# Chunked attention into a GELU MLP: the first tile's V in runs of 512 bytes, with 32-key score and AV blocks

## The chip, the cores and the metric

The kernel runs on one core of one Trainium2 chip. Its time is the device time of one execution in microseconds (us). TensorE is called PE below, its weight loads PEld, VectorE DVE, ScalarE ACT, GpSimd POOL, and SyncE, which issues nearly all transfers, SP.

## The reference

Attention within chunks of 64 tokens, with no mask, and then an MLP with exact GELU over the 4608 tokens:

```python
batch, n_heads, seq, head_dim = (8, 8, 576, 64)
...
scores = scale * np.matmul(q_c, k_c.transpose(0, 1, 2, 4, 3))    # per chunk of 64 tokens
attn = np.exp(scores - max); attn = attn / sum(attn)
out = np.matmul(attn, v_c)
x = out.transpose(0, 2, 1, 3).reshape(B * S, H * D)              # 4608 x 512
h = x @ w_in                                                      # 4608 x 2048
g = 0.5 * h * (1.0 + erf(h * inv_sqrt2))
return g @ w_out                                                  # 4608 x 512
```

Inputs and output are f32 in HBM.

## The kernel before, in words

The 4608 tokens are cut into nine tiles of 512. Tiles 0 to 7 are the first 512 tokens of each batch entry (eight chunks), and the last tile holds the ninth chunk of all eight entries. In each tile attention gives x (four blocks `g` of 128 features, which are two heads each, by 512 tokens), then come the products with w_in (and GELU) and with w_out. Products are in bf16. From tile 1 on, the products use a scheme with seven block products for eight; tile 0 uses plain ones (`mm1_begin` L486, `mm1_slot` L471). Each engine runs its instructions in the order in which the program text issues them (the block under `manual_schedule`, L869). A buffer that is reused makes the writer wait for its last reader.

The change concerns tile 0, that is, L870 to L925. There are no earlier products to hide its attention behind. SP first issues four loads each of q and k (`load_qk`, L112, one pair of heads each), then four of V (`load_v_plain`, L142 to L145), then w_in in chunks (`load_w_in`, L836): the first two chunks in halves, each half in an instruction of its own. w_in's last chunk, w_out and the next tile's q, k and V follow (from L918).

A load puts f32 into a staging tile; POOL, DVE or ACT casts it to bf16 (`cast_qk` L158, `cast_v_plain` L147, `cast` L842). q and k arrive with four consecutive tokens per partition, V with one token per partition: its innermost run in HBM is one row of 64 f32, 256 bytes, and partition p of block n holds key 128 n + p for all heads.

The units of work for each pair of heads `g` are:

- `T[2g]`, `T[2g+1]` (`att_T`, L169): PE transposes q, then k; DVE copies qT and ACT copies kT out of PSUM.
- `att_S` (L371): 16 score matmuls with 64x64 tiles of the PE array (64 features by 64 keys, 64 queries moving). Its PSUM banks hold keys on partitions, one bank per head of the pair. ACT then takes the exponent (L381) into pT.
- The sums over keys are made in two ways. For g = 0 and 1 `att_sum` (L383) multiplies pT by a matrix of ones, so that each sum appears on 64 partitions; DVE transposes 32x32 blocks (L393), takes the reciprocal (L397) and transposes back while spreading it (L398). For g = 2 and 3 `att_sum_pe` (L410) makes one sum per query with queries on partitions (L416), DVE inverts (`inverse`), PE spreads by a product with the identity in f32 (`spread`, L428), and ACT copies to SBUF (L431).
- `att_av` (L434): V is the stationary operand, 64 keys by 64 features, and pT moves. The result for two pairs of heads lies in two PSUM banks, one for each parity `c` of the chunk.
- `att_x` (L445): DVE multiplies by the inverse sums into x (L450).

`keep_warm` (L859) adds matmuls on zeros between the steps. The order of it all is written out by hand (L876 to L917). After the two AV halves of the first four heads and the AV of the last four, `mm1_begin` computes three blocks of h: six matmuls on the first half of x, then six on the second (L491). Its weights are cast by POOL, ACT, POOL (L920 to L923), and DVE casts a fourth (L924). Then `mm1_slot` goes on alone (L481), one block of h after another.

Of the kernel before, what the change touches and what calls it, by code (L numbers as in the profile page):

```python
# [11 lines left out]
def kernel(  # L12
# [37 lines left out]
    ones_bd = consts.tile([P, P], bf16, name="ones_bd")  # L50
    nc.vector.memset(ones_bd[:], 0.0)
    nc.vector.memset(ones_bd[0:CH, 0:CH], 1.0)
    nc.vector.memset(ones_bd[CH:P, CH:P], 1.0)

    ones_r = consts.tile([P, 2], bf16, name="ones_r")
    nc.gpsimd.memset(ones_r[:], 0.0)
    nc.gpsimd.memset(ones_r[0:CH, 0:1], 1.0)
    nc.gpsimd.memset(ones_r[CH:P, 1:2], 1.0)
# [87 lines left out]

    def cast_v_plain(t, copy, ns=range(CT // 2)):  # L147
        st = tiles[t]
        if 0 in ns:
            st["v"] = ld.tile([P, H, CT // 2, D], bf16, tag="v", name="v_nat")  # L150
        for n in ns:
            copy(st["v"][:, :, n], st["vf"][:, :, n])
# [24 lines left out]
    def parity_blocks(ns=range(4)):  # L177

        for n in ns:
            for a in range(2):  # L180
                for r in range(2):
                    c = a ^ r
                    yield n, r, c, 2 * n + c, slice(CH * r, CH * (r + 1)), slice(CH * c, CH * (c + 1))
# [187 lines left out]
    def att_S(t, g):  # L371

        st = tiles[t]
        if g % 2 == 0:
            st["s_ps"] = [ps_at.tile([P, 2, CT // 2, CH], f32, tag="at", name="s_ps") for _ in range(2)]
        for n, r, c, i, rs, cs in parity_blocks():
            nc.tensor.matmul(st["s_ps"][r][cs, g % 2, n], st["kT", g][rs, i, :], st["qT", g][rs, i, :],
                             start=True, stop=True, tile_position=(CH * r, CH * c))
        st["pT", g] = work.tile([P, 2, CT // 2, CH], bf16, tag="pT", name="pT", bufs=4)
        for r in range(2):  # L380
            nc.scalar.activation(st["pT", g][:, r], st["s_ps"][r][:, g % 2], Act.Exp, scale=scale)  # L381

    def att_sum(t, g, later=False):  # L383
        pT = tiles[t]["pT", g]
        sum_ps = ps_at.tile([P, MT], f32, tag="at", name="sum_ps")
        for c in range(2):
            for r in range(2):
                nc.tensor.matmul(sum_ps[CH * r:CH * (r + 1)].rearrange("p (n c e) -> p n c e", c=2, e=CH)[:, :, c],
                                 ones_bd[:, CH * c:CH * (c + 1)], pT[:, r], start=True, stop=True,
                                 tile_position=(0, CH * r))  # L390
# [19 lines left out]
    def att_sum_pe(t, g):  # L410

        pT = tiles[t]["pT", g]
        sT = ps_at.tile([P, 2, MT // P // 2, 2], f32, tag="at", name="sT")
        for r in range(2):
            for m in range(2):
                nc.tensor.matmul(sT[:, r, m], pT[:, r, 2 * m:2 * m + 2].rearrange("p n e -> p (n e)"), ones_r[:],  # L416
                                 start=True, stop=True)
        rr = work.tile([P, 2, MT // P // 2, 2], f32, tag="rr", name="rr", bufs=2)
# [4 lines left out]
        def spread():  # L423
            rc_ps = ps_mm.tile([P, CT // 2, 2, CH], f32, tag="mm", name="rc_ps")
            for m in range(2):
                for c in range(2):
                    for r in range(2):
                        nc.tensor.matmul(rc_ps[CH * r:CH * (r + 1), 2 * m:2 * m + 2, c],  # L428
                                         rr[:, r, m, c:c + 1].to_broadcast([P, D]), ident_f[:],
                                         start=True, stop=True, tile_position=(0, CH * r))  # L430
# [3 lines left out]
    def att_av(t, g2, ns):  # L434

        st = tiles[t]
        pool, tag = ((ps_tp, "tp"), (ps_at, "at"))[g2]
        if 0 in ns:
            st["av", g2] = [pool.tile([P, 2, CT // 2, CH], f32, tag=tag, name="av_ps") for _ in range(2)]
        for g in (2 * g2, 2 * g2 + 1):  # L440
            for n, r, c, i, rs, cs in parity_blocks(ns):
                nc.tensor.matmul(st["av", g2][c][rs, g % 2, n], st["v"][cs, 2 * g + r, n, :], st["pT", g][cs, r, n],
                                 start=True, stop=True, tile_position=(CH * c, CH * r))

    def att_x(t, g2, c, ns):  # L445

        st = tiles[t]
        def part(p):
            return p.rearrange("p g (n c e) -> p g n c e", c=2, e=CH)[:, :, ns[0]:ns[-1] + 1, c]
        nc.vector.tensor_tensor(part(st["x"][:, 2 * g2:2 * g2 + 2]), st["av", g2][c][:, :, ns[0]:ns[-1] + 1],  # L450
                                part(st["rcs", g2][:]), op=mybir.AluOpType.mult)
# [417 lines left out]
    with tc.manual_schedule():  # L869
# [3 lines left out]
        load_v_plain(0)  # L873
# [6 lines left out]
        cast_v_plain(0, PO)  # L880
# [15 lines left out]
        keep_warm(1)  # L896
        att_S(0, 2)
        T[6]()
        r1 = att_sum(0, 1, True)
        T[7]()  # L900
        i2, p2 = att_sum_pe(0, 2)
        i2()
        att_S(0, 3)
# [4 lines left out]
        att_av(0, 0, (0, 1))  # L908
        for c in range(2):
            att_x(0, 0, c, (0, 1))  # L910
        p3()
        att_av(0, 0, (2, 3))
        for c in range(2):
            att_x(0, 0, c, (2, 3))
        att_av(0, 1, range(4))
        for c in range(2):
            att_x(0, 1, c, range(4))  # L917
# [168 lines left out]
```

## Time and profile before

| | |
|---|---|
| median of 3 runs | 274.69 us (274.37 to 274.96) |
| the profiled execution | 274.82 us |
| its span, from the first to the last instruction | 273.0 us |
| granted TensorE clock | 1.00 |
| busy in the span: PE, DVE, ACT, POOL | 260.3, 220.4, 181.8, 91.2 us |
| moved by DMA | 53.96 MB, mean 198 GB/s |

The profile is of one execution. Busy times overlap between engines, so they don't add up to the span. "Idle before" an instruction is the time in which its engine had nothing to do just ahead of it, and behind the arrow stands what ended the wait. In the chain of waits each piece is the work that released the next one; a transfer stands there from its issue to its landing. The ends of matmuls are modelled, and matmuls overlap. In a row of the timeline the first number is the start in us from the start of the span, the second the length of the group, and "x16" is how many instructions it holds.

### The profile page before, as it was taken

To read this page: it belongs to the slowest core of one execution; us is meant where nothing else is said; L and a number is where in the kernel's file an instruction comes from. 1 tells how busy PE (TensorE), PEld (TensorE's weight loads), DVE (VectorE), ACT (ScalarE), POOL (GpSimd) and SP (SyncE) were. 2 spreads that over 40 slices of the span, in tenths; PEclk is the share of its full clock that TensorE was granted. 3 is DMA by queue.
4 is the path that set the end of the run, shared out by engine and by line. 5 is a ranking of instruction groups with operands and counts; after the bars stand their busy time and mean duration, and the time that the engine had idled before them with its cause. 6 is when DMAs were issued, how large, how long until landed. Compare 5 with 4: busy or idle time off the path is not lost.

```text
span 273.0 us, 7454 instructions
## 1 busy us (share of the span) xinstructions
PE 260.3 (95%) x2984; PEld 187.3 (69%) x3009; DVE 220.4 (81%) x386; ACT 181.8 (67%) x353; POOL 91.2 (33%) x180
## 2 busy tenths in 40 slices
PE   8689999999999999999999999999999999999993
PEld 2454454486448644768887888788878887888782
DVE  2663586979796999999989998999899889945852
ACT  3557755788667966986679567946884787338700
POOL 2725667360460443370372355133510321000000
PEclk9999999999999999999999999999999999999999
DMA  6999999996999998999899796987983410130005
GB/s 202 258 359 405 396 394 246 242 268 151 347 222 241 279 176 181 273 231 188 231 265 248 219 249 93 237 192 155 251 121 86 143 41 2 38 111 7 4 0 154
DMA packets 118066, 53.96 MB, mean 198 GB/s; under 512 B 93456, under 2 KB 112912, under 8 KB 118032
## 3 DMA queue, kind: packets, MB, share of 16 engines
q1 hardware_dynamic: 117712, 52.97, 74.8%
q8 instruction: 23, 0.38, 0.6%
q10 hardware_dynamic: 320, 0.52, 0.5%
q14 instruction: 11, 0.09, 0.1%
HBM read 36.70 MB, written 9.44 MB: 169 GB/s over the span
## 4 chain that ended last, share of the span: by engine, by line
PE 80%; DVE 7%; SPq 4%; ACT 3%; DMA 3%; issue 1%; POOL 0%; ACTq 0%; DVEq 0%
PE y_ps L673 27%; PE h_Y L611 11%; PE h_ps L631 8%; PE h_Z L611 8%; PE h_X L611 8%; PE y_ps L771 6%; PE h_ps L481 5%; PE y_ps L795 4%; DMA arrival<-in_moe_w_in_dram 3%; SPq L145 2%; PE s_ps L230 1%; SPq L112 1%; DVE part L255 1%; DVE x L368 1%; ACT y_ps L701 1%
## 5 line engine op out<-in xcount | busy, mean ns | idle before, releaser
L611 PEld LDWEIGHTS <-w_in_s 128*128 128x128 bf16 x384 | 37.4, 98 | 6.8
L673 PEld LDWEIGHTS <-h_s 128*128 128x128 bf16 x384 | 37.0, 98 | 5.4 <-DVE h_s L513 0.8
L673 PE MATMUL y_ps<-w_t,h_s 128*128 128x256 bf16 x288 | 34.7, 273 | 0.3
L611 PEld LDWEIGHTS <-w_in_sb 128*128 128x128 bf16 x288 | 28.1, 98 | 8.3 <-issue 2.0
L208 POOL CAST v_nat<-arrival 128x1024 bf16<-128x1024 f32 x14 | 15.4, 1106 | 53.3 <-DMA arrival<-in_v_dram 46.7
L160 POOL CAST q_nat<-arrival 128x512 bf16<-128x512 f32 x33 | 22.2, 711 | 32.5 <-DMA arrival<-in_q_dram 24.2
L771 PE MATMUL y_ps<-w_out_sb,h 128*128 128x512 bf16 x137 | 31.5, 379 | 1.3 <-issue 1.0
L673 PEld LDWEIGHTS <-h 128*128 128x128 bf16 x288 | 28.2, 98 | 4.7
L631 PE MATMUL h_ps<-x,w_in_sb 128*128 128x512 bf16 x103 | 27.8, 379 | 0.7
L611 PE MATMUL h_Y<-x_t,w_in_s 128*128 128x256 bf16 x192 | 27.6, 272 | 0.0
L611 PE MATMUL h_X<-x,w_in_sb 128*128 128x256 bf16 x192 | 26.8, 273 | 0.0
L655 DVE TENSOR_TENSOR y<-h_Z,y 128x512 f32<-128x512 f32 x32 | 21.6, 680 | 5.8 <-PE h_Z L611 4.9
L160 POOL CAST k_nat<-arrival 128x512 bf16<-128x512 f32 x34 | 22.1, 684 | 11.6 <-DMA arrival<-in_k_dram 7.6
L771 PEld LDWEIGHTS <-h 128*128 128x128 bf16 x144 | 13.4, 98 | 15.6 <-issue 0.8
L673 PE MATMUL y_ps<-w_out_sb,h 128*128 128x256 bf16 x192 | 22.9, 273 | 0.0
L618 ACT ACTIVATE h<-y 128x512 bf16<-128x512 f32 x32 | 20.1, 628 | 1.7 <-DVE y L655 1.6
L867 ACT ACT_TABLE_LOAD x16 | 20.5, 1283 | 1.0 <-PEq L1070 0.7
L644 ACT COPY h_Y<-h_X 128x512 f32<-128x512 f32 x24 | 14.0, 584 | 10.5 <-PE h_X L611 10.4
L255 DVE TENSOR_REDUCE part<-pt 128x16 f32<-128x512 bf16 x28 | 19.2, 686 | 1.0
L633 ACT ACTIVATE h<-h_ps 128x512 bf16<-128x512 f32 x29 | 17.1, 595 | 2.6 <-PE h_ps L631 1.2
L307 DVE TENSOR_TENSOR x<-av_ps,rc 128x512 bf16<-128x512 f32 x28 | 18.0, 670 | 0.6
L631 PEld LDWEIGHTS <-w_in_sb 128*128 128x128 bf16 x116 | 11.4, 98 | 7.7
(129 smaller groups left out, 488.7 us busy)
## 6 DMA issues: line engine op xcount, KB each, us to landing
out_dram<-y_sb SPq DMA_DIRECT2D x32, 256.0 KB, 3.3
arrival<-in_q_dram SPq DMA_DIRECT2D x7, 1024.0 KB, 6.2
arrival<-in_k_dram SPq DMA_DIRECT2D x24, 256.0 KB, 6.2
arrival<-in_v_dram SPq DMA_DIRECT2D x42, 128.0 KB, 3.0
arrival<-in_moe_w_out_dram SPq DMA_DIRECT2D x4, 1024.0 KB, 12.4
arrival<-in_v_dram SPq DMA_DIRECT2D x8, 256.0 KB, 8.3
arrival<-in_moe_w_in_dram SPq DMA_DIRECT2D x4, 512.0 KB, 7.3
arrival<-in_moe_w_in_dram SPq DMA_DIRECT2D x2, 1024.0 KB, 10.4
```

The costliest lines, as they stand in the source:

```text
L160: copy(st[nm][:, g].rearrange("p j r d -> p r j d"), st[nm + "f"][:, 2 * g:2 * g + 2])
L208: copy(st["v"][:, r::2], st["vf"][:, r::2])
L255: nc.vector.tensor_reduce(st["part", g2][:, c, :, :, 0], pt[:].rearrange("p n e u -> p n u e"), axis=mybir.AxisListType.X, op=mybir.AluOpT ...
L307: nc.vector.tensor_tensor(x.rearrange("p n (e u) -> p n e u", u=2), st["av"][g2][c][:].rearrange("p n (e u) -> p n e u", u=2), st["rc", 2 ...
L611: nc.tensor.matmul(banks[g + name][:, i], lhs[:, kk, i], rhs[:, kk], start=fresh and i == kk == 0, stop=(kk == 1), skip_group_check=True)
L618: nc.scalar.activation(h[:, j:j + 2, m], src[:], Act.Gelu)
L631: nc.tensor.matmul(bank[:], w_in_sb[:, ks, f * P:(f + 1) * P], st["x"][:, ks, :], start=(ks == 0), stop=(ks == KS - 1))
L633: nc.scalar.activation(st["h"][:, f, :], bank[:], Act.Gelu)
L655: TT(sums[g, i][:], banks[g + "Z"][:], sums[g, i][:], op=add)
L673: nc.tensor.matmul(out[m], lhs[:, f, m * P:(m + 1) * P], rhs[:, f, :], start=fresh and f == 0 and (m == 0 or len(out) == 3), stop=(f == FH ...
L771: nc.tensor.matmul(y_ps[:], st["h"][:, f, ms * P:(ms + 1) * P], w_out_sb[:, f, :], start=(f == 0), stop=(f == FF - 1))
L867: nc.scalar.activation(act_scratch[:], rest[:, 0:1], func)
```

## The change

V of tile 0 is loaded with two consecutive tokens per partition (`load_v_pairs`), in four loads as before: two halves of the heads by two blocks of 256 tokens. A run in HBM is then 128 f32, 512 bytes. Partition p of block n holds keys 256 n + 2 p + j, for j = 0 and 1. A chunk of 64 keys therefore lies on 32 partitions, once for even and once for odd tokens, and the rest of the attention follows:

- `pair_blocks` takes the place of `parity_blocks`: 32 blocks instead of 16 for each pair of heads. The score matmuls take every other key of a chunk (32 of 64) as stationary operand, in 64x32 tiles of the array.
- `att_sum` has 16 matmuls of 128 columns in place of 4 of 256; even and odd keys are added up in PSUM. `att_sum_pe` keeps its four small matmuls and its eight of the spread; the inverse takes the same number of values.
- AV has 32x64 tiles and adds even and odd keys in PSUM: 128 matmuls for 64. Its result lies in four banks (one for each chunk position `c` of a block) that hold all four pairs of heads, where before each half of the pairs had two banks of its own.
- `att_x` is four multiplies of 256 elements for each two pairs, where before there were four of 256 and two of 512 in all.
- The constants of ones change (`ones_q`), and the cast V tile has rows of 65 elements, of which 64 are used.

In the order, the fourth pair's transposes (`T[6]`, `T[7]`) move ahead of the third pair's scores, and the fourth pair's scores ahead of the third pair's sums. The AV of the first four heads is no longer split around the last spread. Behind this point nothing changes.

```diff
...
     nc.vector.memset(rest[:], 0.0)
     ident = consts.tile([P, P], bf16, name="ident")
     make_identity(nc, ident)
-    ones_bd = consts.tile([P, P], bf16, name="ones_bd")
-    nc.vector.memset(ones_bd[:], 0.0)
-    nc.vector.memset(ones_bd[0:CH, 0:CH], 1.0)
-    nc.vector.memset(ones_bd[CH:P, CH:P], 1.0)
-
-    ones_r = consts.tile([P, 2], bf16, name="ones_r")
-    nc.gpsimd.memset(ones_r[:], 0.0)
-    nc.gpsimd.memset(ones_r[0:CH, 0:1], 1.0)
-    nc.gpsimd.memset(ones_r[CH:P, 1:2], 1.0)
+    Q4 = P // 4
+    ones_q = consts.tile([P, 4], bf16, name="ones_q")
+    nc.vector.memset(ones_q[:], 0.0)
+    for c in range(4):
+        nc.vector.memset(ones_q[Q4 * c:Q4 * (c + 1), c:c + 1], 1.0)
+
     ident_f = consts.tile([P, P], f32, name="ident_f")
     nc.gpsimd.tensor_copy(ident_f[:], ident[:])
     QD = P // G
...
         for n in range(CT // 2):
             nc.sync.dma_start(tiles[t]["vf"][:, :, n], v[t, :, P * n:P * (n + 1), :].rearrange("h key d -> key h d"))
 
+    def load_v_pairs(t):
+        tiles[t]["vf"] = stage_tile()[:].rearrange("p (h n e) -> p h n e", h=H, n=2)
+        for h0 in range(0, H, H // 2):
+            for n in range(2):
+                rows = v[t, h0:h0 + H // 2, 2 * P * n:2 * P * (n + 1), :]
+                nc.sync.dma_start(tiles[t]["vf"][:, h0:h0 + H // 2, n], rows.rearrange("h (p j) d -> p h (j d)", j=2))
+
+    def cast_v_pairs(t, copy):
+        st = tiles[t]
+        st["v"] = ld.tile([P, H, CT // 2, D + 1], bf16, tag="v", name="v_nat")
+        for h0 in range(0, H, H // 2):
+            for n in range(2):
+                copy(st["v"][:, h0:h0 + H // 2, 2 * n:2 * n + 2, :D],
+                     st["vf"][:, h0:h0 + H // 2, n].rearrange("p h (j d) -> p h j d", d=D))
+
     def cast_v_plain(t, copy, ns=range(CT // 2)):
         st = tiles[t]
         if 0 in ns:
...
         copy(xT.rearrange("p i (c j) -> p i c j", j=J), tp)
         tiles[t][nm + "T", g] = xT
 
-    def parity_blocks(ns=range(4)):
-
-        for n in ns:
-            for a in range(2):
-                for r in range(2):
-                    c = a ^ r
-                    yield n, r, c, 2 * n + c, slice(CH * r, CH * (r + 1)), slice(CH * c, CH * (c + 1))
+    def pair_blocks():
+
+        for n in range(2):
+            for j in range(2):
+                for c in range(4):
+                    for r in range(2):
+                        yield n, j, r, c, 4 * n + c, slice(CH * r, CH * (r + 1)), slice(Q4 * c, Q4 * (c + 1))
 
     ORDERED = (0, 1, 3)
 
...
         st = tiles[t]
         if g % 2 == 0:
             st["s_ps"] = [ps_at.tile([P, 2, CT // 2, CH], f32, tag="at", name="s_ps") for _ in range(2)]
-        for n, r, c, i, rs, cs in parity_blocks():
-            nc.tensor.matmul(st["s_ps"][r][cs, g % 2, n], st["kT", g][rs, i, :], st["qT", g][rs, i, :],
-                             start=True, stop=True, tile_position=(CH * r, CH * c))
+        for n, j, r, c, i, rs, cs in pair_blocks():
+            nc.tensor.matmul(st["s_ps"][r][cs, g % 2, 2 * j + n], st["kT", g][rs, i, j::2], st["qT", g][rs, i, :],
+                             start=True, stop=True, tile_position=(CH * r, Q4 * c))
         st["pT", g] = work.tile([P, 2, CT // 2, CH], bf16, tag="pT", name="pT", bufs=4)
         for r in range(2):
             nc.scalar.activation(st["pT", g][:, r], st["s_ps"][r][:, g % 2], Act.Exp, scale=scale)
...
     def att_sum(t, g, later=False):
         pT = tiles[t]["pT", g]
         sum_ps = ps_at.tile([P, MT], f32, tag="at", name="sum_ps")
-        for c in range(2):
-            for r in range(2):
-                nc.tensor.matmul(sum_ps[CH * r:CH * (r + 1)].rearrange("p (n c e) -> p n c e", c=2, e=CH)[:, :, c],
-                                 ones_bd[:, CH * c:CH * (c + 1)], pT[:, r], start=True, stop=True,
-                                 tile_position=(0, CH * r))
+        for c in range(4):
+            for j in range(2):
+                for r in range(2):
+                    nc.tensor.matmul(sum_ps[CH * r:CH * (r + 1)].rearrange("p (n c e) -> p n c e", c=4, e=CH)[:, :, c],
+                                     ones_q[:, c:c + 1].to_broadcast([P, CH]), pT[:, r, 2 * j:2 * j + 2], start=j == 0, stop=j == 1,
+                                     tile_position=(0, CH * r))
         t1 = work.tile([P, NB, 32], f32, tag=f"y_{1 + t}", name="t1", bufs=1)
         rc = rc_of(t, g).rearrange("p (n e) -> p n e", e=32)
         nc.vector.transpose(t1[:], sum_ps[:].rearrange("p (n e) -> p n e", e=32))
...
     def att_sum_pe(t, g):
 
         pT = tiles[t]["pT", g]
-        sT = ps_at.tile([P, 2, MT // P // 2, 2], f32, tag="at", name="sT")
+        sT = ps_at.tile([P, 2, 4], f32, tag="at", name="sT")
         for r in range(2):
-            for m in range(2):
-                nc.tensor.matmul(sT[:, r, m], pT[:, r, 2 * m:2 * m + 2].rearrange("p n e -> p (n e)"), ones_r[:],
-                                 start=True, stop=True)
-        rr = work.tile([P, 2, MT // P // 2, 2], f32, tag="rr", name="rr", bufs=2)
+            for j in range(2):
+                nc.tensor.matmul(sT[:, r], pT[:, r, 2 * j:2 * j + 2].rearrange("p n e -> p (n e)"), ones_q[:],
+                                 start=j == 0, stop=j == 1)
+        rr = work.tile([P, 2, 4], f32, tag="rr", name="rr", bufs=2)
 
         def inverse():
             nc.vector.reciprocal(rr[:], sT[:])
 
         def spread():
-            rc_ps = ps_mm.tile([P, CT // 2, 2, CH], f32, tag="mm", name="rc_ps")
-            for m in range(2):
-                for c in range(2):
-                    for r in range(2):
-                        nc.tensor.matmul(rc_ps[CH * r:CH * (r + 1), 2 * m:2 * m + 2, c],
-                                         rr[:, r, m, c:c + 1].to_broadcast([P, D]), ident_f[:],
-                                         start=True, stop=True, tile_position=(0, CH * r))
+            rc_ps = ps_mm.tile([P, 2, 4, CH], f32, tag="mm", name="rc_ps")
+            for c in range(4):
+                for r in range(2):
+                    nc.tensor.matmul(rc_ps[CH * r:CH * (r + 1), :, c], rr[:, r, c:c + 1].to_broadcast([P, D]), ident_f[:],
+                                     start=True, stop=True, tile_position=(0, CH * r))
             nc.scalar.copy(rc_of(t, g), rc_ps[:].rearrange("p n c e -> p (n c e)"))
         return inverse, spread
 
-    def att_av(t, g2, ns):
-
-        st = tiles[t]
-        pool, tag = ((ps_tp, "tp"), (ps_at, "at"))[g2]
-        if 0 in ns:
-            st["av", g2] = [pool.tile([P, 2, CT // 2, CH], f32, tag=tag, name="av_ps") for _ in range(2)]
+    def att_av(t, g2, n0=0, n1=2):
+
+        st = tiles[t]
+        if "av" not in st:
+            st["av"] = [pool.tile([P, G, 2, CH], f32, tag=tag, name="av_ps")
+                        for pool, tag in ((ps_tp, "tp"), (ps_at, "at")) for _ in range(2)]
         for g in (2 * g2, 2 * g2 + 1):
-            for n, r, c, i, rs, cs in parity_blocks(ns):
-                nc.tensor.matmul(st["av", g2][c][rs, g % 2, n], st["v"][cs, 2 * g + r, n, :], st["pT", g][cs, r, n],
-                                 start=True, stop=True, tile_position=(CH * c, CH * r))
-
-    def att_x(t, g2, c, ns):
-
-        st = tiles[t]
-        def part(p):
-            return p.rearrange("p g (n c e) -> p g n c e", c=2, e=CH)[:, :, ns[0]:ns[-1] + 1, c]
-        nc.vector.tensor_tensor(part(st["x"][:, 2 * g2:2 * g2 + 2]), st["av", g2][c][:, :, ns[0]:ns[-1] + 1],
-                                part(st["rcs", g2][:]), op=mybir.AluOpType.mult)
+            for n, j, r, c, i, rs, cs in pair_blocks():
+                if n0 <= n < n1:
+                    nc.tensor.matmul(st["av"][c][rs, g, n], st["v"][cs, 2 * g + r, 2 * n + j, :D],
+                                     st["pT", g][cs, r, 2 * j + n],
+                                     start=j == 0, stop=j == 1, tile_position=(Q4 * c, CH * r))
+
+    def att_x(t, g2, n0=0, n1=2):
+
+        st = tiles[t]
+        for c in range(4):
+            def part(p):
+                return p.rearrange("p g (n c e) -> p g n c e", c=4, e=CH)[:, :, n0:n1, c]
+            nc.vector.tensor_tensor(part(st["x"][:, 2 * g2:2 * g2 + 2]), st["av"][c][:, 2 * g2:2 * g2 + 2, n0:n1],
+                                    part(st["rcs", g2][:]), op=mybir.AluOpType.mult)
 
     def rc_of(t, g):
 
...
         for g in range(G):
             for nm in "qk":
                 load_qk(0, nm, 2 * g, 2 * g + 2)
-        load_v_plain(0)
+        load_v_pairs(0)
         win = [load_w_in(c, 2 if c < 2 else 1) for c in range(NWC - 1)]
         act_table(Act.Exp)
         keep_warm(7)
         T = att_units(0, DV, AC)
         for nm, g in (("k", 0), ("k", 1), ("q", 2), ("k", 2), ("q", 3), ("k", 3)):
             cast_qk(0, nm, g, PO)
-        cast_v_plain(0, PO)
+        cast_v_pairs(0, PO)
         cast_qk(0, "q", 0, DV)
         T[0]()
         cast_qk(0, "q", 1, DV)
...
         T[5]()
         r0()
         keep_warm(1)
+        T[6]()
+        T[7]()
         att_S(0, 2)
-        T[6]()
         r1 = att_sum(0, 1, True)
-        T[7]()
+        att_S(0, 3)
         i2, p2 = att_sum_pe(0, 2)
         i2()
-        att_S(0, 3)
         r1()
         p2()
         i3, p3 = att_sum_pe(0, 3)
         i3()
-        att_av(0, 0, (0, 1))
-        for c in range(2):
-            att_x(0, 0, c, (0, 1))
+        att_av(0, 0)
+        att_x(0, 0)
         p3()
-        att_av(0, 0, (2, 3))
-        for c in range(2):
-            att_x(0, 0, c, (2, 3))
-        att_av(0, 1, range(4))
-        for c in range(2):
-            att_x(0, 1, c, range(4))
+        for n in range(2):
+            att_av(0, 1, n, n + 1)
+        att_x(0, 1)
         win.append(load_w_in(NWC - 1))
         wout = [load_w_out(0)]
         win[0](0, PO)
```

## The prediction

> **What bounds the kernel now.** I read the totals and the 40 slices of the span first.
>
> ```profile
> span 273.0 us, 7454 instructions
> ...
> PE 260.3 (95%) x2984; PEld 187.3 (69%) x3009; DVE 220.4 (81%) x386; ACT 181.8 (67%) x353; POOL 91.2 (33%) x180
> ...
> PE   8689999999999999999999999999999999999993
> ```
>
> TensorE (PE) is idle for 273.0 - 260.3 = 12.7 us only. Of the slices of 6.8 us, the first three hold the largest holes (busy 8, 6 and 8 tenths, some 5 us idle); behind them it is at 9 tenths or more to the end. So I read the chain of waits for the first 24 us (start, length, what).
>
> ```profile
> 4.83 0.47 SPq L145
> ...
> 10.42 0.85 SPq L145
> ...
> 12.21 6.83 DMA arrival<-in_moe_w_in_dram
> ...
> 19.10 0.63 POOL w_in_sb L843
> 19.72 0.05 issue
> 19.77 1.90 PE h_ps L493 x8
> 21.67 2.37 PE h_ps L481 x11
> ```
>
> Ahead of the first full products at L493 the last wait is a transfer: SP (the queue that issues the loads) is held by the four V loads of L145, the second half of w_in's first chunk is issued behind them at 12.21 and lands 6.83 us later, GpSimd (POOL) casts it, and at 19.77 PE goes on. From 21.67 on PE runs without a gap, so the start of the L481 stretch is the quantity to forecast. I call it M; before, M = 21.67.
>
> The timeline beside it shows a second chain that ends only just earlier.
>
> ```profile
> 15.89 0.76 DVE L450 TENSOR_TENSOR x<-av_ps,rcs 128x256 bf16<-128x256 f32 x2
> 16.51 0.62 POOL L152 CAST v_nat<-arrival 128x512 bf16<-128x512 f32 x1 [2.71 <-DMA arrival<-in_v_dram]
> 17.52 1.95 DVE L450 TENSOR_TENSOR x<-av_ps,rcs 128x256 bf16<-128x256 f32 x4 [0.88 <-PE av_ps L442]
> 18.46 1.04 PE L493 MATMUL h_ps<-x,w_in_sb 128*128 128x512 bf16 x3 [0.74 <-POOL w_in_sb L843]
> 21.50 11.39 PE L481 MATMUL h_ps<-x,w_in_sb 128*128 128x512 bf16 x51
> ```
>
> VectorE (DVE) writes the last of x at 17.52 + 1.95 = 19.47, 0.25 us ahead of the last weight cast (19.10 + 0.63). So removing the transfer alone is worth little: L493 has six matmuls on the first half of x and six on the second; at 11.39 / 51 = 0.22 us each, six after 19.47 end at 20.8, so at most 0.9 us. The change also rebuilds this second chain, and its new length decides.
>
> **The change: transfers.** V is 1 MB either way. The rows of the windows view (last two columns: share of the DMA engines, GB/s) show what 256-byte runs cost.
>
> ```profile
> 6.00:8.00 2.00, 1.23 (x6) 0.23 (x4) 0.73 (x2) 0.18 (x1) 0.46 (x1) 1.00 0.99 342
> ...
> 10.00:12.00 2.00, 1.52 (x42) 0.84 (x40) 1.80 (x4) 1.14 (x3) 1.61 (x3) 1.00 0.76 174
> 12.00:14.00 2.00, 1.26 (x28) 0.82 (x28) 1.33 (x3) 1.24 (x3) 1.23 (x2) 1.00 0.95 222
> ...
> 16.00:18.00 2.00, 1.68 (x64) 1.28 (x64) 1.12 (x4) 0.86 (x3) 0.83 (x2) 1.00 1.06 365
> ...
> 4.83 6.44 SPq L145 DMA_DIRECT2D arrival<-in_v_dram  x4
> ```
>
> Runs of 1 KB (q, k, then w_in) move at 342 to 365 GB/s, the V stretch at 174 to 222, partly because SP is still issuing. With half as many runs the four issues should take about half of 6.44 us, so w_in is issued some 3 us earlier. No 512-byte run is in this trace; the bounds are the V stretch (nothing gained) and the 1 KB rate: 4 us at 342 instead of about 198 moves 0.58 MB more, worth 1.6 us. I take 1.5 us: the second half-chunk is cast by 18.2 rather than 19.73. [...] The four V casts on POOL keep their 512 elements; earlier arrivals put them into POOL's idle 2.71 us.
>
> **The change: attention.** Rows for the pieces:
>
> ```profile
> 3.47 0.43 DVE L160 CAST q_nat<-arrival 128x512 bf16<-128x512 f32 x1 [1.91 <-DMA arrival<-in_q_dram]
> ...
> 9.13 0.67 ACT L381 ACTIVATE pT<-s_ps 128x256 bf16<-128x256 f32 x2
> ...
> 10.16 0.32 PE L377 MATMUL s_ps<-qT,kT 64*64 64x64 bf16 x16
> 10.52 0.66 ACT L381 ACTIVATE pT<-s_ps 128x256 bf16<-128x256 f32 x2 [0.72 <-PE s_ps L377]
> 10.63 0.39 PE L166 MATMUL tp<-ident,k_nat 128*128 128x128 bf16 x4
> 11.07 0.59 ACT L174 COPY kT<-tp 128x512 bf16<-128x512 bf16 x1
> 11.71 0.32 PE L377 MATMUL s_ps<-qT,kT 64*64 64x64 bf16 x16 [0.48 <-ACT kT L174]
> 12.29 0.41 PE L388 MATMUL sum_ps<-pT,ones_bd 128*64 128x256 bf16 x4
> 13.01 0.71 DVE L393 STREAM_TRANSPOSE t<-sum_ps 128x512 f32<-128x512 f32 x1
> 13.77 0.24 PE L416 MATMUL sT<-ones_r,pT 128*128 128x2 bf16 x4 [0.74 <-DVE t L393]
> 14.30 1.09 PE L428 MATMUL rc_ps<-ident_f,rr 128*64 128x128 f32 x16
> 15.33 0.25 PE L416 MATMUL sT<-ones_r,pT 128*128 128x2 bf16 x4
> 15.51 0.32 PE L442 MATMUL av_ps<-pT,v_nat 64*64 64x64 bf16 x16
> 17.02 0.59 ACT L431 COPY rcs<-rc_ps 128x512 f32<-128x512 f32 x1 [0.99 <-PE rc_ps L428]
> 17.76 0.62 ACT L843 CAST w_in_sb<-arrival 128x512 bf16<-128x512 f32 x1
> ...
> 41.70 0.45 PE L330 MATMUL s_ps<-qT,kT 64*64 64x64 bf16 x32
> ```
>
> And from the groups by form, where the mean of one in ns stands behind the busy time:
>
> ```profile
> L450 DVE TENSOR_TENSOR x<-av_ps,rcs 128x256 bf16<-128x256 f32 x4 | 1.5, 420 | 0.9 <-PE av_ps L442 0.9
> ...
> L166 PE MATMUL tp<-ident,k_nat 128*128 128x128 bf16 x12 | 1.2, 221 | 0.6 <-POOL k_nat L160 0.6
> ...
> L388 PE MATMUL sum_ps<-pT,ones_bd 128*64 128x256 bf16 x8 | 1.1, 280 | 0.2 <-ACT pT L381 0.2
> ```
>
> Constants: DVE sets five pieces for four and POOL three fewer, all while DVE waits 1.91 us for the first load; nothing.
>
> Scores: 32 matmuls per pair of heads for 16. The 32 of L330 end after 0.45, the 16 of L377 after 0.32, so 16 more cost 0.13, or 8 ns each. The new tiles are 32 keys wide and are in no row; the bounds are nothing (if eight tiles overlap as four do) and twice this. I take 0.13. Sums (L388): 16 matmuls of 128 columns for 4 of 256, the same columns in all. Four of 256 take 0.41, which two pairs side by side explain (0.28 for one and 0.13 for the next pair). One of 128 columns takes 0.22; eight pairs of half the length, at about 0.055 each, end after 0.22 + 7 x 0.055 = 0.60. The upper bound is L428: 16 matmuls of 128 columns, the same 128x64 stationary shape but in f32, 1.09. I take 0.60, that is +0.19. The per-query sums (L416) keep four matmuls and the spread (L428) eight; both cost the same. AV: 128 matmuls for 64; 64 in a row end after 0.32 + 48 x 0.008 = 0.71.
>
> Now in order, with the starts of before in brackets. The second sum's inputs: the exponents of scores 0 end at 9.80 as before, the first sum's 16 matmuls move scores 1 from 10.16 to 10.38; its exponents start at 10.38 + 0.48 = 10.86 and end at 11.53. The third k transpose still passes in time, its copy on ScalarE (ACT) comes behind the exponents and ends at 12.0 [11.66]. Scores 2 start at 12.05 [11.71]; the fourth pair's transposes, now ahead of them, run while PE waits for this copy, and its k copy fits on ACT ahead of exponent 2, so the move is free there. The second sum starts at 12.43 [12.29] and ends at 13.03; its DVE transpose runs 13.06 to 13.77 [13.01 to 13.72], since DVE no longer has qT of the fourth pair just ahead of it. Scores 3, now ahead of the third pair's sums, have exponent 2 (done 13.2) to wait for; they are off PE at 13.61, before that transpose ends, so they are covered too. Were exponent 2 later by over 0.2 us, every step behind it would move. Per-query sums at 13.82 [13.77], spread 14.35, the next sums 15.38, AV of the first four heads 15.56 [15.51]. To here nothing is won.
>
> Then V is all there, so the 64 AV matmuls run in one go; the first of four DVE multiplies starts at about 16.2. Two of 256 take 0.76 and the four of 17.52 take 1.95; a latency of 0.42 and a step of 0.34 give 1.44 for four. x of the first half is complete at 17.64 [18.28]. The second half's AV writes the same four PSUM banks, and each bank's first write waits for the multiply that reads it: PE stands at the fourth bank until 17.67, where 56 AV matmuls and all of L493 are queued behind it. The spread for the last pair fits ahead (16.2 to 17.3), its ACT copy ends at 17.9 and the ACT weight cast at 18.5. The stalled AV takes about 0.48 and the next multiply starts at 18.25: x ends at 18.25 + 1.44 = 19.69 [19.47]. Six L493 matmuls on the first half run meanwhile (18.2 to 19.5), the other six from 19.73, so M = 19.73 + 1.30 = 21.03, 0.64 us earlier. (DVE's own weight cast follows x and is ready by 20.3.) With the transfers 1.5 us earlier no later weight chunk falls behind PE.
>
> Does the gain last? The next wait of PE on another engine's data that is quoted here is inside the next tile's attention:
>
> ```profile
> 53.33 1.45 PE L481 MATMUL h_ps<-x,w_in_sb 128*128 128x512 bf16 x6 [0.45 <-DVE x L368]
> ```
>
> It hangs on DVE work started by PE itself, so it shifts along. **Sum:** 274.82 - 0.64 = 274.2 for the profiled execution, and for the median, which is 0.13 lower, 274.05. I put it at 274.0.
>
> **Rivals.** *Eight tiles overlap* (chance 0.20): the 16 extra score matmuls and half of the AV ones are free. Scores 1 and 2 give 0.13 each, the two AV blocks 0.2 to 0.25 each: 0.7 more, M near 20.3, 273.4. For it: 16 matmuls of 64 columns in 0.32 already overlap. Against: nothing shows more than four tiles. It then needs the weight cast by 18.4, just inside my 18.2.
>
> *Stationary loads show* (0.25), the case on the other side: the change loads 16 small stationaries per sum for 4 and doubles those of scores and AV. V's rows of 65 elements also put every other load off a 4-byte boundary. If PE can't hide them, each sum is nearer to L428's 1.09, 0.49 more; both sums lie on the chain, so +1.0, M = 22.0, 275.0. If scores and AV take 16 ns a matmul too, scores 1 and 2 add 0.26 each and the AV blocks 0.5 each: +2.5 in all, 276.5. It decides from 0.64 us on. Against it: at 8 ns the 64x64 loads are hidden now. [...]
>
> *The transfers gain nothing* (0.10): w_in still lands at 19.04. The last eight L493 matmuls start at 19.77 as before: M about 21.6, no change, 274.6. Against it are the 174 GB/s stretch and the halved run count.
>
> **How the numbers follow.** The forecast has the remaining 0.45: its own range, from errors of 0.35 us on a dozen steps, is 273.7 to 274.4. About 0.2% (0.55 us) is what a measurement of this kernel can tell from no change; the forecast lies just beyond it, so I give it 0.28 faster and 0.17 same. Eight tiles: 0.20 faster. Loads: 0.10 same, 0.15 slower. Transfers: 0.08 same, 0.02 slower. Together 0.48, 0.35, 0.17. The range goes from 273.2 to 275.5: it leaves out the deeper half of the loads' case and a small tail below.
>
> **What would show it.** V's four issues end before 9 us and the 10 to 14 us window is over 300 GB/s; the second half-chunk is cast before 18.5. Sums take 0.60 and not 1.09, scores 0.45, a 64-matmul AV block 0.71. The wait ahead of L493's second six names DVE x, not POOL w_in. x ends near 19.7 and L481 starts near 21.0. I am wrong if the second sum's DVE transpose starts after 13.4, if AV's stall on the fourth bank is absent, or if M moves and the span doesn't.

## The result: slower, 278.94 us for 274.82

The changed kernel takes 278.94 us (278.21 to 280.04, 4 runs), the kernel before 274.82 on the same chip (274.37 to 275.49, 4 runs): a ratio of 1.0151, 95% interval 1.0109 to 1.0193. The forecast of 274.0 (273.2 to 275.5, slower with a chance of 0.17) was wrong, in its sign too. The profiled execution took 278.21 us with a span of 276.4, which is 3.4 us more than before. Runs of one kernel differ by up to some 2%, and each ratio here is estimated from the faster runs of both kernels, so it need not be the quotient of two medians.

The totals and the slices of the profile after:

```profile
span 276.4 us, 7759 instructions
PE 261.8 (95%) x3136; PEld 189.3 (68%) x3161; DVE 218.3 (79%) x390; ACT 181.6 (66%) x353; POOL 90.7 (33%) x177
PE   7759999999999999999999999999999999999993
PEclk9997999999999999999999999999999999999999
q8 instruction: 24, 0.39, 0.6%
```

Against before, PE has 152 more matmuls and as many more weight loads, and is busy 1.5 us longer. The third slice (13.8 to 20.7 us) is at 5 tenths and the granted clock falls to 7 tenths in the fourth. The loss is in the first 26 us. The chain of waits there (start, length, what):

```profile
12.78 0.73 DVE t L406
13.51 0.04 issue
13.55 0.25 PE sT L429 x4
...
14.09 1.09 PE rc_ps L440 x16
15.19 0.18 PE sT L429 x4
15.37 0.67 PE av_ps L454 x64
16.04 1.41 DVE x L464 x4
17.45 0.04 issue
17.50 0.47 PE av_ps L454 x36
17.96 2.84 issue
20.80 0.38 PE av_ps L454 x18
21.18 0.33 issue
21.52 3.73 PE h_ps L507 x11
25.24 2.81 PE h_ps L495 x13
```

Up to 17.50 us everything comes as forecast or up to 0.3 us earlier. Then PE stops in the middle of the second AV block: 2.84 us in which it waits for nothing that the profile shows ("issue"). No operand is missing, since the 18 matmuls ahead of the gap are of the same line. The long stretch of full products (L495, which was L481) starts at 25.24; before it was 21.67, and the forecast was 21.03.

The timeline shows what did arrive in time, and the windows view the clock behind the stop:

```profile
4.83 4.14 SPq L149 DMA_DIRECT2D arrival<-in_v_dram  x4
11.86 0.32 PE L389 MATMUL s_ps<-qT,kT 64*32 64x64 bf16 x32 [0.16 <-ACT kT L186]
12.10 0.64 PE L401 MATMUL sum_ps<-pT,ones_q 128*64 128x128 bf16 x16
15.30 0.71 PE L454 MATMUL av_ps<-pT,v_nat 32*64 32x64 bf16 x64
16.77 0.62 POOL L857 CAST w_in_sb<-arrival 128x512 bf16<-128x512 f32 x1 [0.67 <-DMA arrival<-in_moe_w_in_dram]
20.80 0.38 PE L454 MATMUL av_ps<-pT,v_nat 32*64 32x64 bf16 x22 [2.84 <-issue]
21.29 1.42 DVE L464 TENSOR_TENSOR x<-av_ps,rcs 128x256 bf16<-128x256 f32 x4 [3.85 <-PE av_ps L454]
25.08 1.24 PE L495 MATMUL h_ps<-x,w_in_sb 128*128 128x512 bf16 x5
```

```profile
10.00:12.00 2.00, 1.84 (x87) 1.29 (x82) 1.65 (x4) 1.33 (x4) 1.69 (x3) 1.00 1.15 346
12.00:14.00 2.00, 1.48 (x84) 1.11 (x68) 1.50 (x5) 1.45 (x5) 1.43 (x3) 1.00 1.10 374
...
18.00:20.00 2.00, 0.00 (x0) 0.00 (x0) 0.00 (x0) 1.67 (x3) 1.09 (x2) 1.00 1.05 400
20.00:22.00 2.00, 0.86 (x24) 0.58 (x26) 0.71 (x3) 0.00 (x0) 0.14 (x1) 0.63 1.05 408
22.00:24.00 2.00, 2.00 (x7) 0.68 (x5) 2.00 (x6) 0.00 (x0) 1.18 (x2) 0.52 1.04 406
```

From 18 to 20 us PE and DVE do nothing, while the DMA engines are full (share 1.05, 400 GB/s). Then the clock is halved (means of 0.63 and 0.52 in the next two windows), and 11 products take 3.73 us, 0.34 each where before one took 0.22. The second half of w_in's chunk had been cast at 17.39; the transfer that bounded the kernel before is 2.3 us earlier, and PE is not there to use it.

### The profile page after: what moved, and what is told of

The parts are those of the page before. It is cut to its first block, busy times and chain, and to the rows that moved or that the text cites. A ratio compares the mean times of both kernels' runs of the same rounds, so it can differ in the third digit from the quotient of the medians.

```text
span 276.4 us, 7759 instructions
## 1 busy us (share of the span) xinstructions
PE 261.8 (95%) x3136; PEld 189.3 (68%) x3161; DVE 218.3 (79%) x390; ACT 181.6 (66%) x353; POOL 90.7 (33%) x177
## 4 chain that ended last, share of the span: by engine, by line
PE 81%; DVE 9%; ACT 3%; issue 3%; DMA 2%; SPq 0%; POOL 0%; DVEq 0%; ACTq 0%
PE y_ps L687 26%; PE h_Y L625 11%; PE h_ps L645 8%; PE h_X L625 8%; PE h_Z L625 8%; PE y_ps L785 6%; PE h_ps L495 5%; PE y_ps L809 4%; DMA arrival<-in_k_dram 2%; PE s_ps L242 1%; PE h_ps L507 1%; DVE part L267 1%; DVE x L380 1%; PE tp L178 1%; ACT h L632 1%
## 5 line engine op out<-in xcount | busy, mean ns | idle before, releaser
L625 PEld LDWEIGHTS <-w_in_sb 128*128 128x128 bf16 x288 | 28.1, 98 | 8.5 <-issue 2.3
L666 DVE COPY y<-h_Y 128x512 f32<-128x512 f32 x16 | 11.0, 686 | 8.8 <-PE h_Y L625 8.1
```

Of the source, the lines that this page charges most:

```text
L625: nc.tensor.matmul(banks[g + name][:, i], lhs[:, kk, i], rhs[:, kk], start=fresh and i == kk == 0, stop=(kk == 1), skip_group_check=True)
```

## What stops PE: a theory, read off the trace

The page's third part has a queue of kind "instruction": q8 moves 24 blocks and 0.39 MB, 16 KB each; before it moved 23. The trace holds 6309 records of PE's instructions (matmuls, weight loads and 12 others) after and 6005 before: a block for about 260 PE instructions in both. So q8 looks like the supply of PE's program. Here are, out of the trace, the first q8 blocks with the number of PE records that had started by then, and PE's gaps over 0.5 us between 12 and 30 us. A gap is counted here from the start of one record to the start of the next, so it is a little longer than the "issue" of the views, which begins at a matmul's modelled end (3.05 for 2.84 us):

```
         q8 block starts (us, took) @ PE records        gaps of PE (start, us) @ PE records
before   13.45 1.94 @206   21.27 0.93 @467              12.81 0.95 @206  17.54 0.92 @445  19.12 0.64 @452
after    12.27 1.00 @330   18.44 0.95 @705              17.75 3.05 @705
```

**Theory F.** PE runs its program in blocks of 256 records: the stops below lie at 449 and 705 (e2_pad20 has both), and 6309 / 24 and 6005 / 23 give some 262 to a q8 block. A bound at 193 is counted back from these and shown by no stop. That the next block is asked for about when PE enters the one ahead of it is the author's guess. After the change record 449 starts at 14.80 us and PE is at 705 at 17.75, 2.95 us later, with the DMA engines moving 388 GB/s: it runs out, and goes on at 20.80, 6.00 us after record 449. Before, record 449 starts at 18.91 and record 705 only at 41.76. Bounds every 256 records from 193 on would be 24 within the records after and 23 before, as many as there are q8 blocks.

**Rival A** puts the stop down to the 32-key AV tiles themselves or the order, **rival T** to w_in's earlier loads as such, whatever PE runs. That the half clock comes first (theory C below) is ruled out by the trace above: PE stops at 17.96, and the clock falls only at 20.50.

## The experiments

In the same sessions the kernel before took 274.66 us (23 runs) for experiments 1 to 4, 274.25 (17 runs) for 5 to 8 and 275.04 (17 runs) for 9 and 10. Experiments 2, 4 and 8 are single runs: they are read for where PE stops, not for their times.

**1 and 2: the count of instructions moved.** `pad` is a small matmul on zeros at the start (64x32 tiles, 64 columns).

```diff
-        keep_warm(7)
+        keep_warm(6)
+        pad_pe(90)        # e1_pad90
```
```diff
         keep_warm(7)
+        pad_pe(20)        # e2_pad20
```

> The changed kernel with 90 small matmuls (180 instructions of PE, on zeros, into a bank that nobody reads) in place of one of the seven warm-up matmuls, that is, before PE's first transpose. Theory F (fetch): PE's instructions come in blocks of about 256 over the transfer engines, a block is asked for when PE enters the one before it, and in the changed kernel PE runs through a whole block of attention in 2.6 us while the fetch needs some 5 us behind the loads; so PE stands for 2.8 us at a fixed count of its instructions and not at a fixed matmul. 180 more instructions ahead move that count into the slow products behind AV: no stall within AV, x ends near 19.7, the L495 stretch starts near 21.0, no half clock, and 274.1 (273.6 to 274.6). Theory A (array): the 32x64 tiles or the four shared banks hold PE up at that place of AV: the stall of 2.8 us stays at the same matmuls and the time is 278 to 279.5. Theory C (only the clock): the half clock comes first and the gap is a by-product: some 278.

> The changed kernel with 20 small matmuls (40 PE instructions) behind the seven warm-up matmuls. Theory F: the gap moves 40 instructions earlier in the program's text, so that some 84 PE records instead of 44 of the second AV block lie behind it, at the same count of about 705 records from the start; its length stays 2.5 to 3.5 us; 278 to 279.5. Theory A: the gap stays in front of the same 44 records, which makes its count 745; same time.

Measured: 277.77 us for the first (275.46 to 280.0, 12 runs; ratio 1.0109, 1.0078 to 1.014) and 276.99 in one run for the second. The timelines of e1_pad90 and e2_pad20:

```profile
15.72 0.42 PE L454 MATMUL av_ps<-pT,v_nat 32*64 32x64 bf16 x33
18.08 0.44 PE L454 MATMUL av_ps<-pT,v_nat 32*64 32x64 bf16 x31 [1.94 <-issue]
20.36 0.80 PE L454 MATMUL av_ps<-pT,v_nat 32*64 32x64 bf16 x64
```

```profile
14.09 0.20 PE L389 MATMUL s_ps<-qT,kT 64*32 64x64 bf16 x2 [1.15 <-issue]
18.92 0.29 PE L454 MATMUL av_ps<-pT,v_nat 32*64 32x64 bf16 x22
20.29 0.53 PE L454 MATMUL av_ps<-pT,v_nat 32*64 32x64 bf16 x42 [1.07 <-issue]
```

The hoped-for "no stall" of e1, with 273.6 to 274.6 us, is a miss: the stop is in the first AV block instead of the second. But it is again at record 705: e1's 90 pads for one warm-up matmul move it 89 matmuls ahead (31 and 64 of AV and the 16 of the last spread are left behind it, where 22 were). In e2 there are two stops, at 449 and 705; with 40 more instructions ahead, 42 AV matmuls are left behind the second instead of 22. That stop is shorter than the 2.5 to 3.5 us expected (1.07), after 1.15 already lost at 449, and e2's time lies below its 278 to 279.5. The place follows the count of instructions and not the work, which speaks for F and against A. In both runs more instructions only moved the bound to an earlier matmul: the 128 AV matmuls with their loads are 256 instructions, so with bounds 256 records apart one falls among them or close by.

**3 and 8: the order.** e3_order is the kernel before with the new order alone, e8_old_order the changed kernel with the old one:

```diff
+        T[6]()
+        T[7]()
         att_S(0, 2)
-        T[6]()
         r1 = att_sum(0, 1, True)
-        T[7]()
+        att_S(0, 3)
         i2, p2 = att_sum_pe(0, 2)
         i2()
-        att_S(0, 3)
```

> The kernel before with only the new order: the fourth pair's transposes ahead of the third pair's scores, and the fourth pair's scores ahead of the third pair's sums. V's load, tiles and AV are as before. By the forecast's working the second sum starts some 0.3 us earlier and its transpose ends at 13.2 instead of 13.72, but the last V cast (17.1) and the second weight half (cast at 19.7) hold the end: L481 starts at 21.5 to 21.7, 274.5 to 274.8, no difference. Theory F agrees (the same number of PE instructions and no block rushed through). If the order is what costs, the time is 276 or more.

> The changed kernel with the order of before (the fourth pair's transposes and scores back behind the third pair's), V's load and tiles as changed. Theory F: the order has no part in the loss; the gap of 2.5 to 4 us stays at 705 records, 278 to 280. Were the new order to blame (scores 3 or its transposes holding a bank or an engine), the gap is gone and the time is 274 to 275.

Measured: the order alone 274.84 us, ratio 0.9979 (0.9939 to 1.0019), no difference that can be told. (Its profiled execution runs at half clock from 8.32 to 15.14 us and stands for 0.58 us, start to start, at record 449.) The changed kernel in the old order takes 278.87 (one run) and stops at record 705 for 2.95 us:

```profile
17.30 1.00 PE L454 MATMUL av_ps<-pT,v_nat 32*64 32x64 bf16 x42
21.04 0.29 PE L454 MATMUL av_ps<-pT,v_nat 32*64 32x64 bf16 x22 [2.74 <-issue]
21.27 4.40 PE L507 MATMUL h_ps<-x,w_in_sb 128*128 128x512 bf16 x12
```

The order is not the cause.

**4: a burst in the kernel before.** 160 small matmuls (the pads, 64x32) between the last spread and the second AV part, whose tiles stay 64x64:

```diff
         p3()
+        pad_pe(160)
         att_av(0, 0, (2, 3))
```

> The kernel before, 64x64 tiles and its own V load, with 160 small matmuls (320 PE instructions on zeros) between the last spread and the second part of AV; they take about 1.1 us themselves. Theory F: the burst makes PE run through a block in under 3 us while w_in is streaming, so PE stands for 2 to 4 us with nothing to wait for at about 705 records, in or just behind the last AV matmuls, and the clock is halved for some 3 us after it: 278 to 281. Theory A: no such tiles are in it, so no gap beyond 1 us, and 275 to 276.

Measured: 282.68 us in one run. Its timeline:

```profile
20.00 0.34 PE L442 MATMUL av_ps<-pT,v_nat 64*64 64x64 bf16 x18
24.75 0.56 PE L442 MATMUL av_ps<-pT,v_nat 64*64 64x64 bf16 x30 [4.40 <-issue]
25.23 4.26 PE L493 MATMUL h_ps<-x,w_in_sb 128*128 128x512 bf16 x12
```

The kernel before, with its own V, its own AV and its own order, stops as well, at record 705 again (a gap of 4.59 us from 20.16, the q8 block at 22.51), and its products behind the stop run at half clock. Stop and time are above what was expected (2 to 4 us, 278 to 281). A, the AV tiles and their banks or the order, falls. The pads are small tiles themselves, so this run alone doesn't clear small tiles in general; e5 below does, with the changed kernel's PE instructions and nearly no stop.

**5, 6 and 7: the load queues emptied.** The loads behind w_in's first chunk are held until ScalarE writes one element into their staging tile: behind the third pair's spread copy (e5_hold_spread, about 15.8 us), behind the last exponent (e6_hold_exp, about 14.2), and in the kernel before likewise (e7_before_hold, 15.1).

```diff
-    def load_w_in(c, parts=1):
+    def load_w_in(c, parts=1, hold=False):
...
+        if hold:
+            nc.scalar.activation(raw[:, 0, 0:1], rest[:, 0:1], Act.Exp)
...
-        win = [load_w_in(c, 2 if c < 2 else 1) for c in range(NWC - 1)]
+        win = [load_w_in(0, 2)]
...
+        win += [load_w_in(1, 2, True), load_w_in(2)]
```

> The changed kernel with the loads behind w_in's first chunk held back: SP waits for a small ACT instruction that stands behind the copy of the third pair's spread (about 15.9 us), so that no bulk load is queued when PE enters its 449th recorded instruction (15.2). Theory F, by which the fetch of the next block stands in line behind the loads (request to use 5.0 to 7 us so far): the fetch starts within 1 us of 15.2 and is usable by 17.7, no gap at 705 records (under 0.5 us), no half clock, L495 starts at 20.8 to 21.3. The loads then run 3 us later; if no wait for weights takes the gap's place, 273.8 to 274.5, else up to 276. If the length of the fetch doesn't come from the loads, the gap of about 3 us at 705 stays: 278 to 280.

> As the one before, but released behind the last exponent (14.2 to 14.4 us), so that about a microsecond of loads is in front of the fetch at 15.2. Theory F: the gap at 705 records is between 0 and 1.5 us, no longer than half of the 3.05 us of the changed kernel; 274 to 276. If the loads aren't the reason: 3 us, 278 to 280.

> The kernel before with the loads behind w_in's first chunk held until its last exponent (15.2 us). If these loads share the transfer engines with w_in's first chunk, as 0.8 MB more moved before its landing than stood ahead of it suggests, the chunk lands at 16.5 to 18 and not at 19.04; then x (19.47) bounds M, L481 starts at 20.7 to 21.0 and the time is 273.7 to 274.2, if the later loads still come in time. If the chunk lands first come first served, M stays at 21.5 to 21.7 and the time at 274.6 to 275. Theory F adds that the gap ahead of L493's seventh record stays absent.

The windows and the timeline of e5_hold_spread, and the same place in e6_hold_exp:

```profile
13.00:15.00 2.00, 1.54 (x21) 1.21 (x22) 1.15 (x4) 0.66 (x2) 0.44 (x1) 1.00 0.86 299
15.00:17.00 2.00, 2.00 (x89) 1.69 (x89) 1.32 (x5) 0.75 (x3) 0.89 (x2) 1.00 0.13 38
```

```profile
18.34 0.29 PE L454 MATMUL av_ps<-pT,v_nat 32*64 32x64 bf16 x22 [0.52 <-issue]
18.57 1.47 PE L507 MATMUL h_ps<-x,w_in_sb 128*128 128x512 bf16 x6
20.25 1.46 PE L507 MATMUL h_ps<-x,w_in_sb 128*128 128x512 bf16 x6 [0.22 <-DVE x L464]
```

```profile
20.24 0.38 PE L454 MATMUL av_ps<-pT,v_nat 32*64 32x64 bf16 x22 [2.35 <-issue]
```

With the DMA engines at 38 GB/s from 15 to 17 us, the q8 block starts at 15.73 instead of 18.44 and PE's gap at record 705 is 0.72 us instead of 3.05. The clock stays at 1.00 and L495 starts at 21.55 (expected: a gap under 0.5, 20.8 to 21.3). PE's instructions are the same; only the bulk loads are missing. In e6, where the loads run again 1.6 us earlier, the gap is 2.56 us. So the wait is for a block that comes behind bulk loads. But e6 is a miss as well: 0 to 1.5 us was expected, and loads that started again at 14.22, only 0.5 us ahead of record 449 (14.72), cost nearly the whole wait. The block doesn't simply wait for the loads issued ahead of it; how it gets its turn, and whether it waits for the DMA engines or for HBM, is open.

The traces add two things. In all ten stops at a bound (in nine of the runs), PE goes on 1.2 to 1.5 us after the end of a q8 block. And where no load moves, the block is early: in e6 at 233 us, with 0 GB/s, its transfer begins 1.7 us and 22 records before the bound's record starts, where under loads it begins 3.1 to 3.8 us after record 449 in the seven runs that stop for over 1 us at 705.

The time does not come back with it: 278.25 us (ratio 1.0103, 1.0051 to 1.0155) for e5 and 278.16 (1.012, 1.0072 to 1.0167) for e6. So no run shows that the whole loss goes with the stop. e5's runs lie far apart (275.15, 276.21, and four from 278.08 to 280.82 us), and the profiled one is the longest. In it PE stands for 1.81 us at 65 us and 2.72 at 122 us, with half clock from 125.03 to 128.44, none of which the changed kernel has; the first ends with a late transfer of the next tile's k (`k_t<-k_nat`), whose loads now start later. What costs the other runs their time is open. In the kernel before, holding changes nothing (274.51, ratio 0.9994, 0.996 to 1.0028), where 273.7 to 274.2 was expected: the chunk ahead of the held loads landed no earlier (19.31 us for 19.04).

**9 and 10: the two halves of the change apart.** e9_v_only is the kernel before with V's loads and casts of the change, e10_blocks_only the changed kernel with those of before.

```diff
-        load_v_plain(0)
+        load_v_pairs(0)
...
-        cast_v_plain(0, PO)
+        cast_v_pairs(0, PO)
```

> The kernel before with V's loads and casts of the change alone (512-byte runs; scores, sums and AV keep their 64x64 tiles and their order). Keys and V's rows no longer belong together in this kernel; the work is the same. Theory F (the small tiles issue PE's instructions faster than they are fetched): the count of PE's instructions is that of before (6005 records), it passes record 449 at about 18 and reaches 705 only behind 33 us, so there is no stall; w_in's second half is cast by 17.4 as in the changed kernel, the last wait is x (19.0 to 19.5), M = 20.3 to 20.9, time 273.3 to 274.0, ratio 0.995 to 0.998. Rival T (the loads of w_in that start 2.3 us earlier, with the DMA engines full from 10 us on, do the harm whatever PE runs): a stall of 2 to 3 us and 277 or more. Rival N (w_in's arrival never decided): M = 21.5, no difference.

> The changed kernel with V's loads and casts of before (256-byte runs, one token per partition), 32-key tiles and order as changed. Keys and V's rows no longer belong together in this kernel; the work is the same. Theory F: PE's instruction records are those of the changed kernel, so PE stops again at record 705, in the second AV block; AV starts later (V's last cast ends near 17.1), which covers part of the wait: a stall of 1 to 3 us, half clock behind it, L495 from 23.5 to 25.5, time 276.5 to 279. Rival T (the early loads do the harm): no stall, L495 from 21.5 to 22, 274.5 to 275.

Measured: V's loads alone 274.08 us (272.99 to 278.03, 12 runs) beside 275.04 (17 runs), ratio 0.9986 (0.9944 to 1.0028); the small tiles alone 279.98 (4 runs), ratio 1.0168 (1.0118 to 1.0218). e9 is just above the 273.3 to 274.0 expected, e10 above its 276.5 to 279. The product of the two, 1.0154, agrees with the 1.0151 of the whole change, within wide intervals. V's rows have 64 elements in both, so the change's rows of 65 have no part in e10's stop. The timeline of e9_v_only, and the chain of e10_blocks_only:

```profile
16.73 1.95 DVE L465 TENSOR_TENSOR x<-av_ps,rcs 128x256 bf16<-128x256 f32 x4 [0.64 <-PE av_ps L457]
17.54 2.75 PE L508 MATMUL h_ps<-x,w_in_sb 128*128 128x512 bf16 x11 [0.61 <-DVE x L465]
20.12 7.07 PE L496 MATMUL h_ps<-x,w_in_sb 128*128 128x512 bf16 x32
```

```profile
17.48 1.41 DVE x L464 x4
18.89 0.04 issue
18.93 0.47 PE av_ps L454 x36
19.40 2.45 issue
21.85 0.44 PE av_ps L454 x22
```

With V's loads alone the transfer's gain is there: no stop, the full products from 20.12 instead of 21.50 in the same view before, the span 271.9 instead of 273.0. In the times it is too small to be told from nothing. T falls. The small tiles with the old V stop at record 705, from 19.19 us on for 2.66 (a stretch of half clock from 9.69 to 13.10 makes the whole chain of this execution some 1.4 us later than after); their span is 278.2. So the stop comes with the small tiles' instructions and not with the new loads.

## Why the prediction was wrong, step by step

- **The step that failed** is "The stalled AV takes about 0.48", and with it the six products that "run meanwhile (18.2 to 19.5)". The sum took PE to issue whatever stands in its queue. PE was held at the fourth bank as forecast (until 17.50, forecast 17.67), then did 36 more matmuls (the chain's count) in 0.47 us, and, by theory F, ran out of program: AV ends at 21.18 instead of 18.15, 3.03 us late, 2.84 of it the stop. The experiments show that the stop belongs to a record count (1, 2, 4), comes with the small tiles and not with V's loads (9, 10), and shrinks when the load queues are empty (5).
- **The rest of the loss** is in its wake: from AV's end to L495 4.06 us instead of 2.88, which is 0.33 of a second issue gap (its cause is open) and about 0.85 that the products at half clock explain. 3.03 + 1.18 = 4.21 = 25.24 - 21.03. The span carries it to the end: 276.4 against the 272.4 that the forecast implies (273.0 - 0.64).
- **The rivals** held none of this. "Stationary loads show" had the sign, by another mechanism, and is refuted: the second sum took 0.64 us and not 1.09, and the first 0.88, of which 0.28 is a wait for the second exponent, as before. "Transfers gain nothing" is refuted by 17.39 for the cast and by e9. "Eight tiles overlap" was right on its term for the scores, 0.32 for 32 matmuls as for 16 (the forecast had 0.45), and wrong for AV (64 in 0.71, as the forecast had). Changes in instruction count were priced in PE time alone; that 304 more instructions are also fetched was not considered, though q8 stood in the page.
- **Transfers:** right, and mis-sized on the safe side. V's four issues take 4.14 us and not half of 6.44, but end at 8.97 (before 9 was asked), the 10 to 14 us windows have 346 and 374 GB/s (over 300), the second half-chunk is cast at 17.39 (forecast 18.2). The 346 is the rate of V's 512-byte runs: from 10 to 12 us nearly all that moves is these, 1326 of them beside 13 of 1 KB. The 374 has more of w_in's 1 KB runs in it (625 beside 177).
- **Attention to 17.5 us:** right within 0.3 us. Sums 0.64 (forecast 0.60), second transpose on DVE 12.78 (13.06), per-query sums 13.55 (13.82), AV 15.30 (15.56), x's first half 16.02 to 17.44 (16.2 to 17.64). The moved transposes and scores cost nothing, as said; experiment 3 agrees.
- **x's second half** starts at 21.29 (forecast 18.25) and takes the 1.42 forecast as 1.44. **"M moves and the span doesn't"** was named as what would prove me wrong; M and the span moved together, but the other way.
- **What a measurement can tell** was put at 0.2%. The intervals here are 0.3 to 0.5% to each side, so even the forecast 0.64 us could hardly have been told from no change.

## What to carry to other kernels

Cutting matmuls into smaller tiles costs instructions even where PE's own time doesn't grow (32 score matmuls with 32 weight loads in 0.32 us here, where 16 with 16 took the same): ask how many PE instructions (weight loads count) run in that stage within the time that the next q8 block took behind loads, here 5.5 to 6.2 us from record 449 to PE's going on at 705. 256 in 2.95 us with the DMA engines moving 388 GB/s was too fast here; in the kernel before, whose next 256 take 22.85 us (18.91 to 41.76), most of it 0.22 us products, nothing stopped at 705. A gap put down to "issue" with all operands there is to be looked up against the "instruction" queue of the page.

## What the runs showed of the hardware

- The q8 block that came behind bulk loads (343 to 430 GB/s from 10 to 22 us after) was late. In the seven runs that stop for over 1 us at 705, PE goes on 5.5 to 6.2 us after record 449 has started (in e1 12.31 to 18.08), and in e5, with the loads held, after 3.7. The block's own transfer takes 0.9 to 1.3 us there (0.95 after, 18.44 to 19.39); the rest is waiting, and 1.2 to 1.5 us from its end to PE's next instruction (19.39 to 20.80 after). The moment of asking is inferred and is in no record. The stops at 449 and 705 lie 256 records apart, and the one at 705 cost 2.84 us after and 4.40 in e4.
- The stops of 3.05 us after and 4.59 in e4 were followed by 3.41 us at a granted clock of 0.5 (20.50 to 23.92 after, 24.89 to 28.31 in e4). Of e2's two shorter ones, 1.34 and 1.26 us from start to start, the first was followed by such a stretch (15.04 to 18.45) and the second by none, and the 0.72 us gap of e5 by none. A stop isn't the only thing in front of a half clock: e3 has it from 8.32 to 15.14 us without such a stop.
- 32 score matmuls of 64x32 tiles end in the time of 16 of 64x64 (0.32 us in three of the four groups after; the fourth takes 0.59), with 32 weight loads for 16.
